# Sigmoid attention and a maxout block on one core: decodes in other visits, weight splits and two sums at other steps

## The chip, the cores and the metric

The program runs on one core of a Trainium2 chip. Times are microseconds (us) of device time; the result is the median of several runs. The engines are TensorE (PE), VectorE (DVE), ScalarE (ACT), GpSimd (POOL) and SyncE (SP), which issues nearly all DMAs from one queue, in order.

## The reference, cut to what matters

```python
scores = scale * np.matmul(q, k.transpose(0, 1, 3, 2)) - np.log(S)   # 8 batches, 12 heads, 448 x 64
attn = 1.0 / (1.0 + np.exp(-scores))
x = np.matmul(attn, v)            # laid out as 3584 tokens x 768
h = np.maximum(np.maximum(x @ w1, x @ w2), x @ w3)
return h @ w_out                  # all weights 768 x 768
```

## The kernel before, in words

Each engine works through its own list in the order in which the program writes it (`keep_in_program_order`), so an instruction that waits holds up everything behind it on its engine. All large products are made of float32 operands split into a high part (a ScalarE copy that rounds) and a low part (a VectorE subtraction, operand minus high part), and three matmuls take the place of one.

The program has three stretches. First comes the attention. Then come the three products of the maxout block, as Strassen-like products with twelve **visits** (`visits`, numbered here from 0): three rounds over four pairs of token blocks, the rounds using other quarters of the weights. A visit has 21 **steps** r, each one product of nine matmuls: seven products k for each of the three weights q, interleaved by the list `order` so that products k5 and k6 of one weight come after k0 of the next. `put` (L801) reads finished banks of PSUM: products k3 and k6 by a copy or a maximum, k4 and k5 by adding `p3`, which is VectorE work at L809, or at L814 and L815. Product k6 goes into the same bank as k4 and may only begin when k4's bank has been read; two products (k0 and k5 of others) lie between the two. Visit 0 has 19 steps.

Weights arrive in a coded form as 64-bit words. `decoding` (L196) loads three coded tiles ahead and turns one at a time into float32: two ScalarE passes (L220, L221) and four VectorE operations (L222, L226, L230, L231) by way of the tile `wb`, of which there is one. For rounds 1 and 2 the result is stored to DRAM by SP (L248), and the next decode's first VectorE operation cannot begin before this store has landed. The last twelve decodes, for the last layer's weights, write another tile and store nothing there. The table `decodes` (L778) says after which step of which visit a decode is written; `todo` says what is decoded in which order: first one tile for round 1 (which the load at visit 3, step 19 needs), then twelve for round 2 (the first four needed at visit 6), then twelve for the last layer. In the first four visits POOL makes the token sums of the next visit, some four us after another, beside this work.

The last stretch is the last layer, `h @ w_out`, with a scheme of 15 products (`STEPS`) of which each has two halves q of six matmuls; four pairs v of token blocks give 60 layer steps g. A product takes four blocks of 128x128 of the combined weights, 60 blocks in 20 tiles j of three blocks each, so layer step g < 15 needs tiles up to (4g+3)//3. Chains A, B and C of steps accumulate in the same banks without clearing them; `l_take` (L907) reads the bank after each step (L926 by ScalarE, L930 by VectorE), and the next step of the chain, often two steps later, must wait for that read. Token operands are h blocks b0 to B1, loaded by SP, and POOL sums of two (`X_SUMS`, 128x896; v's sums s0 to s16).

The work of the last layer is written by a plan with **places**: places 0 to 20 are the last 21 products (visit 11 from step 2 on), and layer step g is place 21 + g; a place's plan is written behind the product (places 0 to 20) or ahead of it (layer steps). In the plan stand, in this order: low part of a weight tile (`wl_lo`, L724), low part of a token operand (`l_lo`, L708), high part of one (`l_hi`, L698), POOL sums (`l_sum`, L676), loads (`l_load`, L671), high part of a weight tile (`wl_hi`, L720) and its load (L716). For layer step g the high part is written at place 18 + g and the low part at place 19 + g, but for those in the table EARLY; the operand goes into one of four sets, so the high part for step g waits until step g - 4 is done. `room` says for which steps ScalarE also copies the operand into the one PSUM buffer `ps_av` (L701), from which `l_lo` then reads instead of from SBUF. WL_SPLITS gives the place of each tile's high part; the low part follows one place later. `l_take_raw` (L658) hands out buffers for loads and sums from a list of free ones, by its order.

Of the kernel before, what the change touches and what calls it, by code (L numbers as in the profile page):

```python
# [101 lines left out]
def attention_then_maxout(  # L102
# [90 lines left out]
    def raw_tile(dec_p, name, words=HP):  # L193
        return dec_p.tile([P, words], I64, name=name, bufs=1)
# [457 lines left out]
    slots = ["xs_b11", "xs_t2", "xs_b12", "xs_b21", "xs_t1", "xs_t4", "xs_b22"]  # L652
# [3 lines left out]
    plan = {}  # L656

    def l_take_raw(key):  # L658
        name = slots.pop(0)
        if name[:2] == "wr":  # L660
            t = raw_tile(dec_p, name, S).bitcast(F32).rearrange("p (a s) -> p a s", s=S)
        elif name[:2] == "xs":
            t = xs_p[name == "xs_t4"].tile([P, HALF, S], F32, name=name)
        else:
            t = xo_p[1].tile([P, HALF, S], F32R, name=name).bitcast(F32)
        l_raw[key] = t[:, :2], name

    def l_load(v, name):
        l_take_raw((v, name))
        j, th = divmod(int(name[1]), 2)  # L670
        pin(nc.sync.dma_start(out=l_raw[v, name][0], in_=h_dram[v][:, th, j]))  # L671

    def l_sum(v, name):
        l_take_raw((v, name))
        a, b = (l_raw[v, x][0] for x in X_SUMS[name])
        pin(nc.gpsimd.tensor_tensor(out=l_raw[v, name][0], in0=a, in1=b, op=ALU.subtract))  # L676


    ROOM = (4, 7, 9, 10, 11, 12, 14, 0, 1)

    def room(v, s):
        return s in ROOM and (v or s > 4)

    def l_hi(v, s):
        g, x = v * len(STEPS) + s, l_raw[v, STEPS[s][1]][0]
        if g:
            name = SETS[(g - 1) % len(SETS)]
            to = xo_p[name not in FIRST]
            hi, lo = (
                to.tile([P, HALF, S], F32R, name=f"x{part}_{name}")[:, :2] for part in ("hi", "lo")  # L690
            )
        else:
            both = wl_p[0].tile([P, len(L_SUMS) * P], F32R, name="sums")
            hi, lo = (
                both[:, k * 2 * S : (k + 1) * 2 * S].rearrange("p (a s) -> p a s", a=2)
                for k in range(2)
            )
        pin(nc.scalar.copy(out=hi, in_=x))  # L698
        if room(v, s):
            px = ps_av.tile([P, 2, 512], F32, name="ps_av")  # L700
            pin(nc.scalar.copy(out=px[:, :, :S], in_=x))  # L701
            x = px[:, :, :S]
        l_ops[g], l_px[g] = (hi, lo), x
# [8 lines left out]
    def wl_load(j):  # L712
        q, k = divmod(j, len(PRODUCTS))
        wl_ops[j] = w_tiles(q, PRODUCTS[k][0])
        src = wl_dram[:].rearrange("p s b c -> p (s b c)")[:, j * HP : (j + 1) * HP]
        pin(nc.sync.dma_start(out=wl_ops[j][1].bitcast(F32), in_=src))  # L716
# [12 lines left out]
    for v in pairs:  # L729
        for s, (_, x, *_) in enumerate(STEPS):  # L730
            events.append((v, s - 3, 1, l_hi, s, (x,)))
            events.append((v, s - 2, 0, l_lo, s, () if room(v, s) else (x,)))
        events += [(v, s, 2, l_sum, x, X_SUMS[x]) for s, x in X_AT.items()]
        events += [(v, s, 3, l_load, x, ()) for s, xs_ in LOADS.items() for x in xs_]
# [4 lines left out]
        (l_load, "b5"): 5, (l_load, "b4"): 7,  # L739
        (l_sum, "s7"): 3, (l_sum, "s0"): 5, (l_sum, "s2"): 7, (l_sum, "s3"): 8,  # L740
        (l_sum, "s6"): 10, (l_sum, "s15"): 12,
        (l_hi, 0): 7, (l_hi, 1): 13, (l_hi, 2): 16, (l_hi, 3): 17, (l_hi, 4): 18,
        (l_lo, 0): 8, (l_lo, 1): 14, (l_lo, 2): 17, (l_lo, 3): 18, (l_lo, 4): 19,
    }

    def place(v, s, _, run, what, *rest):
# [18 lines left out]
    for k, e in enumerate(events):  # L765
        plan.setdefault(place(*e), []).append(lambda k=k: l_event(k))
    WL_LOADS = (1, 2, 3, 4, 5, 7, 8, 8, 9, 10, 11, 12, 14, 15, 15, 16, 17, 18, 19, 20)
    WL_SPLITS = (6, 7, 8, 9, 10, 11, 12, 13, 14, 15, 16, 17, 18, 19, 19, 20, 22, 24, 24, 26)
    for j, (at, split_at) in enumerate(zip(WL_LOADS, WL_SPLITS)):
        plan.setdefault(at, []).append(lambda j=j: wl_load(j))  # L770
        plan.setdefault(split_at, []).append(lambda j=j: wl_hi(j))
# [3 lines left out]
        for run in plan.get(at, ()):  # L775
            run()

    decodes = {n: (8, 11) if n < 3 else (6, 8, 10) for n in (1, 2, 3, 4, 5, 6, 8, 9, 10)}  # L778
    decodes = [(n, r) for n in decodes for r in decodes[n]]
    todo = [(1, 2, 3)] + [(2, q, n) for q in range(3) for n in range(4)]  # L780
    todo += [(STAGES, u, n) for u in range(2) for n in range(2 * HALF)]
# [39 lines left out]
    for at, (n, r, old, q, k) in enumerate(order):  # L821
# [21 lines left out]
        if here in his:  # L843
            to, name = his.pop(here)
# [8 lines left out]
        if here in x_loads:  # L853
            to, name = x_loads.pop(here)
# [87 lines left out]
    for g in range(end + 1):  # L942
        v, s = divmod(g, len(STEPS))
# [53 lines left out]
```

## Time and profile before

| | before |
|---|---|
| median of 3 runs | 857.94 us (857.68 to 858.5) |
| the profiled execution | 858.38 us, span 856.6 us, 1.8 us around it |
| PE busy | 846.0 us, 99% of the span, 5410 matmuls |
| VectorE, ScalarE, POOL busy | 618.7 us (72%), 510.5 us (60%), 238.8 us (28%) |
| chain that ended last | PE 95%, VectorE 4%, issue 1% |
| attention, visits, last layer | to 245.7 us, to 703.3 us, to 856.6 us |

PE's busy time includes matmuls that overlap in the pipeline; whether PE waited is seen from the starts of its matmuls, which follow one another at a fixed distance while nothing is late. A row of the timeline gives start, duration, engine, line, tiles and shapes, and in brackets the idle time before it with what ended it.

### The profile page before, as it was taken

Reading aid. Unit: us, or ns where it says so; the run is one execution under the profiler, and the core shown is the slowest. Engines: PE = TensorE matmul, PEld = TensorE weight load, DVE = VectorE, ACT = ScalarE, POOL = GpSimd, SP = SyncE. Lnnn points to the kernel's source line nnn. Section 1 sums busy time; section 2 is a strip of 40 time slices with the busy share of each in tenths; the row PEclk is TensorE's granted clock in tenths of the full one; section 3 lists DMA queues with packets and bytes.
Section 4 is the critical chain, followed back from the end, with each engine's and each line's share of the span. In section 5 each row is a group of like instructions: output and inputs, shape, how many; then the busy total and the mean of one; then the engine's idle time right before and its main releaser. Section 6 shows DMA issues by size and latency. Waiting matters only on the chain.

```text
span 856.6 us, 14461 instructions
## 1 busy us (share of the span) xinstructions
PE 846.0 (99%) x5410; PEld 699.0 (82%) x5410; DVE 618.7 (72%) x820; ACT 510.5 (60%) x717; POOL 238.8 (28%) x192
## 2 busy tenths in 40 slices
PE   9999999999999999999999999999999998999998
PEld 5555555555579989899999999999999987999997
DVE  5678668877883786875675765567576699898885
ACT  6888888888872444443364443345444445777774
POOL 0010020112017257204000230330303545578660
PEclk9999999999999999999999999999999999999999
DMA  8666777786666546446583922458382723735413
GB/s 295 209 211 228 252 247 232 259 298 239 196 248 224 205 177 226 180 124 210 196 268 116 326 71 66 163 197 281 123 294 67 249 90 126 237 132 190 151 65 129
DMA packets 79878, 166.95 MB, mean 195 GB/s; under 512 B 7616, under 2 KB 55744, under 8 KB 79808
## 3 DMA queue, kind: packets, MB, share of 16 engines
q1 hardware_dynamic: 79664, 165.92, 56.4%
q8 instruction: 42, 0.69, 0.3%
q14 instruction: 28, 0.23, 0.1%
q10 hardware_dynamic: 144, 0.11, 0.0%
HBM read 113.31 MB, written 52.69 MB: 194 GB/s over the span
## 4 chain that ended last, share of the span: by engine, by line
PE 95%; DVE 4%; issue 1%; DMA 0%; ACT 0%; DVEq 0%
PE ps_y L598 50%; PE ps_y L887 16%; PE ps_s L437 9%; PE ps_s L461 7%; PE ps_av L461 6%; PE ps_s L472 2%; PE ps_s L450 2%; PE ps_av L437 2%; DVE wb L226 1%; DVE wb L230 1%; DVE xlo_t L708 1%; DVE wb L231 0%; DMA w_dram<-wb 0%; PE ps_s L508 0%; DVE wb L222 0%
## 5 line engine op out<-in xcount | busy, mean ns | idle before, releaser
L799 ACT COPY ps_y<-ps_y 128x448 f32<-128x448 f32 x72 | 37.3, 518 | 170.1 <-PE ps_y L598 146.0
L407 ACT ACTIVATE a<-ps_s,bias_s 128x896 f32<-128x896 f32 x121 | 114.6, 1017 | 10.7 <-PE ps_s L437 10.7
L598 PE MATMUL ps_y<-xhi_t,whi_s 128*128 128x448 f32 x324 | 117.5, 363 | 0.0
L598 PE MATMUL ps_y<-xlo_t,whi_s 128*128 128x448 f32 x324 | 117.4, 362 | 0.0
L598 PE MATMUL ps_y<-xhi_t,wlo_s 128*128 128x448 f32 x324 | 116.8, 361 | 0.0
L178 POOL TENSOR_TENSOR ws_s<-ws_a,ws_a 128x384 f32<-128x384 f32 x9 | 9.7, 1080 | 285.7 <-DMA ws_a<-w_dram 180.1
L598 PE MATMUL ps_y<-xhi_b,whi_a 128*128 128x448 f32 x216 | 78.3, 362 | 0.0
L598 PE MATMUL ps_y<-xlo_b,whi_a 128*128 128x448 f32 x216 | 78.3, 362 | 0.0
L598 PE MATMUL ps_y<-xhi_b,wlo_a 128*128 128x448 f32 x216 | 78.0, 361 | 0.0
L598 PEld LDWEIGHTS ps_y<-xlo_t,whi_s 128*128 128x128 f32 x324 | 60.8, 188 | 4.4
L598 PEld LDWEIGHTS ps_y<-xhi_t,wlo_s 128*128 128x128 f32 x324 | 60.6, 187 | 4.2
L598 PEld LDWEIGHTS ps_y<-xhi_t,whi_s 128*128 128x128 f32 x324 | 60.8, 188 | 3.5
L461 PE MATMUL ps_av<-a,v 64*64 64x448 f32 x576 | 62.6, 536 | 0.0
L356 DVE TENSOR_TENSOR xlo_t<-xs_t,xhi_t 128x1344 fp32r<-128x1344 f32 x30 | 47.5, 1586 | 17.3 <-ACT xhi_t L352 15.4
L461 PE MATMUL ps_s<-a,v 64*64 64x448 f32 x576 | 59.7, 545 | 0.0
L814 DVE TENSOR_TENSOR c<-ps_y,p 128x448 f32<-128x448 f32 x48 | 29.8, 621 | 35.4 <-PE ps_y L598 35.3
L419 DVE TENSOR_TENSOR lo<-qk,hi 128x896 fp32r<-128x896 f32 (+4 forms) x51 | 53.5, 1049 | 1.8
L356 DVE TENSOR_TENSOR xlo_b<-xs_b,xhi_b 128x1344 fp32r<-128x1344 f32 x30 | 49.4, 1648 | 0.0
L352 ACT CAST xhi_t<-xs_t 128x1344 fp32r<-128x1344 f32 x30 | 39.6, 1320 | 15.1 <-PE ps_y L598 15.1
L461 PEld LDWEIGHTS ps_av<-a,v 64*64 64x64 f32 x576 | 22.0, 133 | 32.1 <-issue 32.1
L437 PE MATMUL ps_s<-hi 64*128 64x448 f32 x240 | 46.4, 384 | 0.0
L809 DVE TENSOR_TENSOR m<-ps_y,p 128x448 f32<-128x448 f32 x24 | 15.0, 624 | 42.0 <-PE ps_y L598 18.7
(214 smaller groups left out, 2225.4 us busy)
## 6 DMA issues: line engine op xcount, KB each, us to landing
qk<-qk SPq DMA_DIRECT2D x47, 448.0 KB, 4.7
xs_b<-x_dram SPq DMA_DIRECT2D x30, 672.0 KB, 6.4
wraw<-w SPq DMA_DIRECT2D x36, 384.0 KB, 4.5
xs_t<-t_dram SPq DMA_DIRECT2D x18, 672.0 KB, 6.9
v<-v SPq DMA_DIRECT2D x24, 448.0 KB, 5.5
h_dram<-m SPq DMA_DIRECT2D x48, 224.0 KB, 2.1
x_dram<-m SPq DMA_DIRECT2D x47, 224.0 KB, 2.9
t_dram<-xs_t SPq DMA_DIRECT2D x12, 672.0 KB, 3.8
```

The source lines that it names most:

```text
L352: pin(copy(out=hi, in_=r[name]))
L356: pin(nc.vector.tensor_tensor(out=lo, in0=x, in1=hi.bitcast(F32), op=ALU.subtract))
L407: pin(nc.scalar.activation(out=a, in_=banks[:, :, :S], func=AF.Sigmoid, bias=bias_s, scale=scale))
L419: pin(nc.vector.tensor_tensor(out=lo[:, cols], in0=t[:, cols], in1=high.bitcast(F32), op=ALU.subtract))
L437: pin(nc.tensor.matmul(bank[e][:, :S], kt[r, S + c * P : S + (c + 1) * P], qt[r, :S], start=n == 0, stop=n == len(terms) - 1,))
L450: pin(nc.tensor.matmul(ps[g * D : (g + 1) * D, e, :S], t[r, S + C * P :], t[r, :S], start=True, stop=True,))
L461: pin(nc.tensor.matmul(ps[e * D : (e + 1) * D, :S], vt[rows, (g * C + c) * 2 + e], chunks[c][rows, e], start=c == 0 and not (ahead and r = ...
L472: pin(nc.tensor.matmul(ps[e * D : (e + 1) * D, :S], vt[r, 4 * C + e], a[r, e], start=ahead[g], stop=not ahead[g],))
L598: pin(nc.tensor.matmul(ps[:, :S], wt[:, k * P : (k + 1) * P], xt[:, k], start=first and n == 0, stop=n == len(terms) - 1, skip_group_check ...
L799: pin(nc.scalar.copy(out=bank(cycle, b)[:, :S], in_=y[:, :S]))
L814: pin(nc.vector.tensor_tensor(out=c, in0=y, in1=add, op=ALU.add))
L887: pin(nc.tensor.matmul(ps[:, :S], wl_ops[j][part][:, c * P : (c + 1) * P], xt[:, k], start=first and m == 0, stop=m == len(terms) - 1, ski ...
```

## The change

Four edits in tables and one in the choice of buffers. No arithmetic changes; the number of decodes (25), of weight tiles (20) and of POOL sums stays.

- Decodes: visits 1 and 2 had two each, after steps 8 and 11. Now visits 0, 1 and 2 have one each, after steps 10, 8 and 8, and visit 5 has four (a new one after step 12). Visits 3, 4, 6, 8, 9 and 10 keep theirs.
- Weight tiles 0 to 13 of the last layer are split one or two places earlier; tiles 14 to 19 go from places 19 to 26 to places 28 to 33.
- The operand of layer step 0 is split one place earlier.
- For the first pair, steps 11 and 12 no longer copy their operand into PSUM.
- The sums s8 and s16 of the first pair take the buffer that was freed last, not first.

```diff
-        name = slots.pop(0)
+        name = slots.pop(-1 if key in ((0, "s8"), (0, "s16")) else 0)
...
-        return s in ROOM and (v or s > 4)
+        return s in (ROOM if v else (7, 9, 10, 14))
...
-        (l_hi, 0): 7, (l_hi, 1): 13, (l_hi, 2): 16, (l_hi, 3): 17, (l_hi, 4): 18,
-        (l_lo, 0): 8, (l_lo, 1): 14, (l_lo, 2): 17, (l_lo, 3): 18, (l_lo, 4): 19,
+        (l_hi, 0): 6, (l_hi, 1): 13, (l_hi, 2): 16, (l_hi, 3): 17, (l_hi, 4): 18,
+        (l_lo, 0): 7, (l_lo, 1): 14, (l_lo, 2): 17, (l_lo, 3): 18, (l_lo, 4): 19,
...
-    WL_SPLITS = (6, 7, 8, 9, 10, 11, 12, 13, 14, 15, 16, 17, 18, 19, 19, 20, 22, 24, 24, 26)
+    WL_SPLITS = (4, 5, 6, 7, 8, 10, 11, 11, 12, 13, 14, 15, 17, 18, 28, 29, 30, 31, 32, 33)
...
-    decodes = {n: (8, 11) if n < 3 else (6, 8, 10) for n in (1, 2, 3, 4, 5, 6, 8, 9, 10)}
+    decodes = {n: (6, 8, 10) for n in (3, 4, 5, 6, 8, 9, 10)}
+    decodes = {0: (10,), 1: (8,), 2: (8,), **decodes, 5: (6, 8, 10, 12)}
```

## Rows read from the trace of the kernel before

**Rows 1.** Windows without stall and behind the longest: us, busy (instructions) by engine, granted clock, DMA.

```profile
349.00:660.00 311.00, 311.00 (x1555) 291.51 (x1556) 202.64 (x288) 140.93 (x219) 51.28 (x80) 1.00 0.54 182
721.20:724.40 3.20, 3.20 (x9) 2.85 (x10) 3.20 (x5) 0.91 (x1) 1.80 (x1) 0.51 0.00 0
```

**Rows 2.** Timeline of PE at its six stalls: start, us, instruction, idle before.

```profile
308.57 0.36 PE L598 MATMUL ps_y<-xhi_t,whi_a 128*128 128x448 f32 x1
...
310.38 0.36 PE L598 MATMUL ps_y<-xlo_b,whi_s 128*128 128x448 f32 x1
...
347.79 0.37 PE L598 MATMUL ps_y<-xhi_t,whi_a 128*128 128x448 f32 x1
...
349.24 0.37 PE L598 MATMUL ps_y<-xlo_b,whi_s 128*128 128x448 f32 x1
...
689.05 0.37 PE L598 MATMUL ps_y<-xhi_t,whi_a 128*128 128x448 f32 x1
...
689.74 0.37 PE L598 MATMUL ps_y<-xlo_b,whi_s 128*128 128x448 f32 x1
...
700.14 0.37 PE L598 MATMUL ps_y<-xhi_t,whi_a 128*128 128x448 f32 x1
...
701.69 0.36 PE L598 MATMUL ps_y<-xlo_b,whi_s 128*128 128x448 f32 x1
...
707.89 0.37 PE L887 MATMUL ps_y<-xhi_b,whi_s 128*128 128x448 f32 x1
...
708.68 0.36 PE L887 MATMUL ps_y<-xlo_t,whi_s 128*128 128x448 f32 x1
...
718.08 0.36 PE L887 MATMUL ps_y<-xhi_t,wlo_s 128*128 128x448 f32 x1
721.10 0.60 PE L887 MATMUL ps_y<-xlo_t,whi_s 128*128 128x448 f32 x1 [2.65 <-DVE xlo_t L708]
...
724.79 0.37 PE L887 MATMUL ps_y<-xhi_t,whi_s 128*128 128x448 f32 x1
```

**Rows 3.** Timeline of VectorE, visit 1: second decode, then the late read of a bank.

```profile
304.30 0.36 DVE L222 TENSOR_SCALAR wb<-wraw 128x384 uint32<-128x384 uint32 x1 [2.05 <-DMA w_dram<-wb]
...
309.41 0.61 DVE L814 TENSOR_TENSOR c<-ps_y,p 128x448 f32<-128x448 f32 x1
```

**Rows 4.** Timeline of VectorE, visit 0: a long idle stretch.

```profile
265.82 0.62 DVE L811 TENSOR_TENSOR m<-ps_y,m 128x448 f32<-128x448 f32 x1 [6.63 <-PE ps_y L598]
```

**Rows 5.** Timeline of VectorE, visit 5: first and last operation of the third decode.

```profile
456.60 0.36 DVE L222 TENSOR_SCALAR wb<-wraw 128x384 uint32<-128x384 uint32 x1 [1.98 <-DMA w_dram<-wb]
...
458.28 0.56 DVE L231 SCALAR_TENSOR_TENSOR wb<-c,wb 128x384 f32<-128x384 f32 x1
```

**Rows 6.** Waits of VectorE for a store: us in total, times, longest.

```profile
DVE wb L222 <- DMA w_dram<-wb: 12.5, 6, 2.9
```

**Rows 7.** Timeline of VectorE, visit 11: reads of banks ahead of place 14.

```profile
686.36 0.61 DVE L811 TENSOR_TENSOR m<-ps_y,m 128x448 f32<-128x448 f32 x1
...
688.76 0.61 DVE L814 TENSOR_TENSOR c<-ps_y,p 128x448 f32<-128x448 f32 x1
```

**Rows 8.** Timeline of VectorE in the last layer: two-input operations, then one from PSUM.

```profile
715.66 2.49 DVE L724 TENSOR_TENSOR wlo_a<-wlo_a,whi_a 128x384 fp32r<-128x384 f32 x1
718.07 2.97 DVE L708 TENSOR_TENSOR xlo_t<-xs_t,xhi_t 128x896 fp32r<-128x896 f32 x1
...
722.03 1.08 DVE L708 TENSOR_TENSOR xlo_t<-ps_av,xhi_t 128x896 fp32r<-128x896 f32 x1
```

**Rows 9.** Timeline of POOL in the last layer: one sum under VectorE traffic, one alone.

```profile
715.29 2.44 POOL L676 TENSOR_TENSOR xlo_t<-wraw,xs_b 128x896 f32<-128x896 f32 x1
...
737.01 2.15 POOL L676 TENSOR_TENSOR xs_t<-xs_b,xhi_t 128x896 f32<-128x896 f32 x1 [10.12 <-ACT ps_av L701]
```

**Rows 10.** Timeline of ScalarE in the last layer: a high half.

```profile
714.03 0.96 ACT L698 CAST xhi_t<-xs_b 128x896 fp32r<-128x896 f32 x1
```

**Rows 11.** DMA issues: count, KB each, median us from issue to landing.

```profile
xs_b<-h_dram SPq DMA_DIRECT2D x10, 448.0 KB, 5.8
```

## The prediction

> **What bounds the kernel now.** I read the summary first: PE is busy for 99% of the span and the chain that ended last is PE for 95%, so only what makes PE wait counts. The view of windows shows what PE does when nothing is late: 1555 matmuls in 311.00 us, one every 0.200 us [rows 1]. A product of a visit (nine matmuls) is thus 1.80 us and a layer step (twelve) 2.40 us. Next I went through the starts of PE's matmuls from the end of the attention on and looked for distances over 0.22 us. There are six places, and each costs the distance from the last matmul before to the first one at full pace, less 0.200 for each interval between [rows 2]: in visits 1 and 2, 1.41 and 1.05 us; in visit 11 at places 14 and 20, 0.29 and 1.15; in the last layer ahead of step 2, 0.39, and inside step 6, 4.51 (11 intervals), where 2.65 us of idleness are followed by slow matmuls, at a granted clock of 0.51, the lower of its two levels, 1.2 GHz [rows 1]. Together 8.80 us. Everything else on PE is work that the change does not touch, so the floor is 857.94 - 8.80 = 849.1 us. All six waits end with a VectorE operation: five with the L814 or L811 that frees a bank, one with a token's low part. VectorE's list is what has to be followed.
>
> **Decodes.** In visit 1 the second decode begins at 304.30, 2.05 us after VectorE was ready, because the one `wb` was still being stored; L814, which frees the bank for k6, ends at 310.02 behind it, and PE starts at 310.07 [rows 2, 3]. Visit 2 repeats it. With one decode in these visits nothing stands between the first decode (done by 302.3) and L814, whose product ends at 305.2, two products ahead of the last matmul before k6: both waits go, -2.46. The decode that moves to visit 0, step 10 meets a VectorE that idles 6.63 us up to 265.82 [rows 4]. Beside POOL's sums, as in visit 1, a decode took at most the 4.6 us from 304.30 to the reads of banks ahead of 309.41 [rows 3], so it fits; were it a little late, L814's bank is due only 3.6 us after its product. Nothing, then; if that cover were gone, 1 us as in visit 2. Its store goes on SP's queue ahead of token stores that wait for POOL's sums anyway. The load that came with the decode at step 11 now comes at step 8 and has a whole visit to land.
>
> Visit 5 gets a fourth decode between k3's and k4's reads. The third decode ends at 458.84, and a decode takes 2.24 us from first to last [rows 5]. The gap ahead of the third decode, the wait for the second's store, was 1.98 [rows 5]; with it the fourth runs from 460.82 to 463.06, L814 (0.61 [rows 7]) follows to 463.67, and k6, due at 462.45 (63 products behind the one whose second matmul is that of 349.24 [rows 2]), starts at 463.7. With 0.1 for the restart as in the other stalls that is **+1.35**; bounds 0.9 (an overlap of the operations as dense as 0.48 us each) and 2.3 (a gap of 2.9, the longest of the six such waits [rows 6]). It is a wait for a DMA in VectorE's list, and behind it stand exactly the reads that PE needs. The Trainium skill's page "DMA: Bandwidth & Descriptors", section "Anatomy of one DMA", gives about 2.0 us fixed plus bytes over 436 GB/s for a DMA issued by GpSimd, an estimate of 2.45 for a store of 192 KB; by it the wait would be near 0.5 longer. The measured gap of 1.98 decides, and the sum keeps 1.35.
>
> **Visit 11.** ScalarE's and VectorE's weight splits for tiles 0 to 13 come earlier, tiles 14 to 19 go. Ahead of place 14, VectorE still has to do the same number of two-input operations (three low parts of weights and one of a token) in the time in which POOL makes its sums one after another, and each of them waits for the end of a running sum. What changes is that L811 now stands behind the last of them, not before: in the trace it ran at 686.36 while POOL held the next low part back anyway, and L814 began at 688.76 [rows 7]. Now L814 ends about 0.53 later, near 689.9 against a due time of 689.25: 0.70 + 0.11 = **0.81** in place of 0.29 (bounds 0.2 and 1.5). Behind it POOL is idle, as s8 is held back, three low parts of weights are missing, and L814 at place 20 ends 1 us early: the 1.15 and the 0.39 go.
>
> **The last layer.** This is where the change puts work, and the cover must be looked at. What the trace shows of VectorE beside POOL: a low part from PSUM takes 1.08 us whatever POOL does; one with both inputs in SBUF, of the same shape, took 2.97, and a 128x384 weight part 2.49 [rows 8]. Both ended just behind the end of a POOL sum: they start when the running sum ends, and POOL's next sum waits for them (2.44 under such traffic, 2.15 alone [rows 9]). So while POOL has sums ready, VectorE gets one two-input operation for each sum. The Trainium skill's "GPSIMD Engine Reference", section "Key points", says that the two share SBUF interfaces and contend where VectorE has two SBUF inputs; it has no price. It speaks against this change; without it the layer would have no wait.
>
> Let u be the time from the start of layer step 0. Step g is due at 2.4 g; the high part for g begins at 2.4 (g - 3) + 0.2 (0.96 [rows 10], then about as long for the copy into PSUM). Step 6 is safe now: its low part stands behind no weight part and ends at 9.9, due at 14.4: -4.51. But s8 now takes the buffer that ScalarE frees with the PSUM copy for step 7, at 12.0, and s16 that which the low part for step 8 frees, at 15.3 (VectorE first waits for s8 to end). POOL then has s16, s11, s5, s7, s0 and s2 (the last three for the next pair) in a row from 15.4, at about 2.1 each, into u = 30; in the trace this chain began before step 5. Into this stretch fall the low parts of tiles 14 to 19 and, without their PSUM copies, those for steps 11 and 12, and then 13. In order:
>
> - tile 14's high part follows the PSUM copy for step 10 and ends at 20.05; its low part waits for s5's end at 21.75. Then the low part for step 10 (PSUM) and two bank reads, to 24.3.
> - tile 15's low part gets in at s7's end, 24.2; the one for step 11 waits for s0's end, 26.6, and ends at 27.6; the bank read of step 9 follows. Step 11 starts at 28.2, due 26.4: 1.8 late.
> - tile 16 at 29.5; the one for step 12 from 29.95 to 31.0: 2.25 late. Between them POOL's next sum is not ready, as its load, issued at 24.8 behind the output of step 8, needs 5.8 [rows 11].
> - tile 17 behind that sum, 33.4, used at 32.85: 2.8 late; step 13's from 35.35 to 36.4: 5.25 late; tile 18 at 38.75, used at 37.65: 6.4 late; tile 19, whose high part waits for a PSUM copy that waits for step 14's low part, at 43.25, used at 40.6: **9.1 late**.
>
> After that no weight parts are left, and 7 us between high part and use absorb single waits as they did in the trace. The bounds of 9.1: 0.4 if VectorE finds POOL idle each time; 12.5 if tile 15 misses s7's end, which it makes by 0.1, so that all behind it slips by a sum. The clock may fall after a wait of over 2 us as it did after 2.65, but slow matmuls there mostly fill the next wait.
>
> **The sum**, against the profiled execution's 858.38: less 8.80, plus 1.35, 0.81 and 9.1, gives 860.84. The median of the runs is 0.44 below that execution, so I predict **860.4**. As a formula: 851.3 plus the layer's wait.
>
> **The rivals.**
> 1. VectorE's operations slip in between POOL's sums, at the 1.08 us or less that an undisturbed VectorE needs [rows 8], because the sums' loads or buffers come later than I think and leave gaps. Then the layer waits 0 to 4: 851.3 to 855.3, faster. It decides at the low part for step 11: if it is done by u = 26.4, this holds. For it: the trace has 7 us between high part and use and no wait of this kind in the later pairs, where POOL is as busy. Against it: there no weight parts stand in the list, and the critical steps have PSUM copies.
> 2. Some of the waits come and some not, above all if the loads for s3 and s6 of the next pair land later than 7 us and POOL pauses in steps 12 and 13: 4 to 8, 855.3 to 859.3.
> 3. All slips by one sum (tile 15 misses): 12.5 and perhaps a stretch at the low clock: 861.8 to 865.
> 4. The decode in visit 5 costs nothing, its store landing sooner: -1.35 on any of these. That the edits do not do what they say I exclude: they are tables.
>
> **How the numbers follow.** The forecast (8 to 10.5 in the layer, 859.3 to 861.8, its own range) has 0.33, rival 1 has 0.28, rival 2 0.22, rival 3 0.17. The range goes from 853.0, which leaves out about 0.12 of rival 1, to 864.0, which leaves out 0.04. A measurement of this kernel tells 0.2% (1.7 us) from no change; no change is thus 856.2 to 859.7. Slower: rival 3 and most of the forecast, 0.47. Same: a part of the forecast and most of rival 2, 0.20. Faster: rival 1 and the low end of rival 2, 0.33.
>
> **What would show it right or wrong.** In the changed kernel's trace: no stall in visits 0, 1 and 2; one of 1.2 to 1.5 us in visit 5 ahead of k6, ended by L814 with L222 behind a store; one near 0.8 at place 14 and none at place 20; none in layer step 6. POOL's sums s16 to s2 in one row across layer steps 6 to 12, and low parts of 2.4 and 3.0 us there; PE waiting for L708 and L724 in steps 11 to 14. I am wrong if POOL shows gaps in that stretch or if the low part for step 11 is done before step 10 ends.

## The result and the profile after

| | before | changed |
|---|---|---|
| median, in runs on the same chip | 857.81 us | 863.06 us (862.6 to 865.95) |
| ratio | | 1.0069, interval 1.0045 to 1.0093 |
| the profiled execution | 858.38 us, span 856.6 | 862.89 us, span 861.1 |
| PE's waits in visits 1 and 2 / visit 5 / place 14 / place 20 | 2.46 / 0 / 0.29 / 1.15 us | 0 / 1.10 / 0.95 / 0 us |
| PE's wait in the last layer | 4.90 us (steps 2 and 6) | 11.06 us (steps 11 to 14) |

The changed kernel is slower by 0.7%. PE's waits are those of the profiled execution. Lines have moved by one or two: L889 is the last layer's matmul (L887 before), L709 the low part of a token (L708), L725 that of a weight tile (L724), L816 the read of a bank with `p3` (L814), L932 the bank read of the layer (L930), L677 a POOL sum (L676), L702 the copy into PSUM (L701), L721 the high part of a weight tile (L720).

The timeline of PE at five of the stalls of the changed kernel, for each the last matmul ahead and the first behind, with what ended the wait in brackets: most lie in the last layer, and there a bank read, a token's low part and a weight's low part take turns. A stall costs the distance of the two starts, less 0.20, and about 0.1 for the restart:

```profile
460.00 0.36 PE L598 MATMUL ps_y<-xhi_t,whi_a 128*128 128x448 f32 x1
461.19 0.47 PE L598 MATMUL ps_y<-xhi_b,wlo_s 128*128 128x448 f32 x1 [0.83 <-DVE c L816]
...
687.90 0.37 PE L598 MATMUL ps_y<-xhi_t,whi_a 128*128 128x448 f32 x1
688.95 0.47 PE L598 MATMUL ps_y<-xhi_b,wlo_s 128*128 128x448 f32 x1 [0.68 <-DVE c L816]
...
727.86 0.37 PE L889 MATMUL ps_y<-xhi_t,whi_a 128*128 128x448 f32 x1
729.90 0.45 PE L889 MATMUL ps_y<-xhi_t,wlo_a 128*128 128x448 f32 x1 [1.68 <-DVE m L932]
...
732.39 0.37 PE L889 MATMUL ps_y<-xhi_b,wlo_s 128*128 128x448 f32 x1
734.62 0.47 PE L889 MATMUL ps_y<-xlo_b,whi_s 128*128 128x448 f32 x1 [1.86 <-DVE xlo_b L709]
...
745.47 0.58 PE L889 MATMUL ps_y<-xhi_t,whi_s 128*128 128x448 f32 x1
746.80 0.47 PE L889 MATMUL ps_y<-xhi_t,wlo_a 128*128 128x448 f32 x1 [0.76 <-DVE wlo_a L725]
```

460.00 to 461.19 is visit 5 (1.10), 687.90 to 688.95 place 14 (0.95). Layer step 0 starts at 701.66, so 729.90 is u = 28.24, the start of step 11, due at 26.4. Step 12 stops after its first matmul (732.39 to 734.62), and the last wait of the row, 746.80, is inside step 14, for tile 19; between the two lie further waits for tile 17, step 13 and tile 18, which are not shown. From there on every step is 11.06 us late and stays so. Nothing is late in visits 1 and 2, at place 20, or in layer steps 0 to 10. The remaining 0.2 us of the difference between the spans is that the visits start later, as the attention took longer in this execution.

VectorE in the last layer, beside POOL's sums (start, us, operation):

```profile
725.74 0.55 DVE L725 TENSOR_TENSOR wlo_s<-wlo_s,whi_s 128x384 fp32r<-128x384 f32 x1
726.21 3.02 DVE L709 TENSOR_TENSOR xlo_t<-xs_t,xhi_t 128x896 fp32r<-128x896 f32 x1
...
730.21 1.41 DVE L725 TENSOR_TENSOR wlo_s<-wlo_s,whi_s 128x384 fp32r<-128x384 f32 x1
731.54 3.02 DVE L709 TENSOR_TENSOR xlo_b<-xhi_t,xhi_b 128x896 fp32r<-128x896 f32 x1
734.49 2.46 DVE L725 TENSOR_TENSOR wlo_a<-wlo_a,whi_a 128x384 fp32r<-128x384 f32 x1
736.88 2.98 DVE L709 TENSOR_TENSOR xlo_b<-wraw,xhi_b 128x896 fp32r<-128x896 f32 x1
...
744.69 2.06 DVE L725 TENSOR_TENSOR wlo_a<-wlo_a,whi_a 128x384 fp32r<-128x384 f32 x1 [0.36 <-ACT whi_a L721]
```

```profile
723.30 2.45 POOL L677 TENSOR_TENSOR xhi_t<-wraw,xs_b 128x896 f32<-128x896 f32 x1
725.83 2.45 POOL L677 TENSOR_TENSOR xlo_t<-xhi_t,xlo_t 128x896 f32<-128x896 f32 x1
728.24 2.97 POOL L677 TENSOR_TENSOR xs_t<-wraw,xlo_t 128x896 f32<-128x896 f32 x1
731.17 2.45 POOL L677 TENSOR_TENSOR xs_b<-xlo_b,wraw 128x896 f32<-128x896 f32 x1
733.58 2.96 POOL L677 TENSOR_TENSOR wraw<-xs_b,xhi_b 128x896 f32<-128x896 f32 x1
736.62 2.30 POOL L677 TENSOR_TENSOR xs_b<-wraw,xhi_t 128x896 f32<-128x896 f32 x1
```

These are the rows that answer to [rows 8, 9]. 726.21 is the low part for layer step 11. POOL's sum had begun at 725.83 and ended at 728.28; the low part took 3.02 us and ended at 729.23, 0.95 behind the end of the sum; and POOL's next sum took 2.97 in place of the 2.15 of [rows 9], as it waited for the low part. The same happens at 730.21 (tile 16, up for the last 1.00 us of that sum), 731.54 (step 12), 734.49 (tile 17) and 736.88 (step 13). Only the tile 15 part at 725.74 found the gap between two sums and took 0.55. Here VectorE gets one such operation for each sum, as [rows 8] had suggested. The Trainium skill's "SBUF — State Buffer", section "SBUF: two separate sides", states a rule for this: of a VectorE instruction with two SBUF inputs and a GpSimd one that reads SBUF, whichever starts first has the shared access for the whole instruction, and the other is blocked fully. The trace agrees, to 0.13 us: 3.02 is the rest of the running sum, 2.07 (726.21 to 728.28), and 0.95 behind it, where the operation takes 1.08 undisturbed.

### The profile page after: what moved, and what is told of

Its sections match the earlier page's. It is cut to its first block, busy times and chain, and to the rows that moved or that the text cites. A ratio compares the mean times of both kernels' runs of the same rounds, so it can differ in the third digit from the quotient of the medians.

```text
span 861.1 us, 14454 instructions
## 1 busy us (share of the span) xinstructions
PE 848.9 (99%) x5410; PEld 700.2 (81%) x5410; DVE 618.8 (72%) x820; ACT 508.5 (59%) x715; POOL 240.0 (28%) x192
## 5 line engine op out<-in xcount | busy, mean ns | idle before, releaser
L816 DVE TENSOR_TENSOR c<-ps_y,p 128x448 f32<-128x448 f32 x48 | 29.9, 622 | 38.0 <-PE ps_y L598 36.9
L230 DVE CUSTOM_DVE_ANT_0 wb<-wraw,wb 128x768 uint16<-128x768 uint16 x48 | 28.6, 597 | 22.3 <-ACT wraw L221 18.7
```

Source lines behind the costliest of these rows:

```text
L230: pin(nc.vector.tensor_tensor(out=bits, in0=bits, in1=low, op=ALU.add))
L816: pin(nc.vector.tensor_tensor(out=c, in0=y, in1=add, op=ALU.add))
```

## The experiments

### The two halves of the change alone: d_only and l_only

d_only is the kernel before with the new decodes; l_only the changed kernel with the old ones.

```diff
-    decodes = {n: (8, 11) if n < 3 else (6, 8, 10) for n in (1, 2, 3, 4, 5, 6, 8, 9, 10)}
+    decodes = {n: (6, 8, 10) for n in (3, 4, 5, 6, 8, 9, 10)}
+    decodes = {0: (10,), 1: (8,), 2: (8,), **decodes, 5: (6, 8, 10, 12)}
```

d_only:

> Only the decodes move (one each in visits 0, 1 and 2, four in visit 5); the last layer is that of before. Both theories of the last layer expect the same here: the waits of visits 1 and 2 (1.41 and 1.05 us) are gone, one of about 1.1 to 1.35 stands in visit 5 ahead of k6, and the layer keeps its 0.39 and 4.51. Time: 857.8 - 2.46 + 1.1 to 1.35 = 856.4 to 856.7 us, ratio near 0.9985. A rival to the account of the fourth decode (its store lands in time and it costs nothing) expects 855.4.

l_only (all other edits of the change):

> Only the last layer's edits (splits, PSUM copies, buffers of s8 and s16); the decodes are those of before. If the parts add up: 857.8 plus 6.15 in the layer (11.06 in place of 4.91) and less 0.5 at places 14 and 20, 863.4 us, ratio near 1.0066. If the loss came from an interaction with the decodes, it is below 862.

Measured: d_only 855.68 us, ratio 0.9986 (0.9974 to 0.9997); l_only 864.08 us, ratio 1.0079 (1.0065 to 1.0094); the kernel before had 857.5 us in these runs. The loss is all in the last layer's edits. d_only's median is 1.8 us below that of the kernel before, which is more than the 1.1 to 1.4 expected, and not all of it is the edit's. Visits 1 and 2 have no stall and visit 5 has one of 1.88, not 1.1 to 1.35, so in this profile the decodes give 2.46 - 1.88 = 0.6. The two profiles lie 3.3 us apart (855.07 and 858.38): 1.6 of that is the clock, as the next rows show, 0.8 an attention that ended earlier, and 0.3 the stall of place 14, which is missing here. In l_only PE stands still in visits 1 and 2 (1.15 and 0.88), step 11 is 1.85 late and the layer's wait 12.71 us.

The profile of d_only shows one thing more, in layer step 6, which this edit does not touch. The timeline of PE, and the view of windows behind the stall (us, busy of PE, PEld, VectorE, ScalarE, POOL, granted clock, DMA share and GB/s):

```profile
716.40 0.37 PE L888 MATMUL ps_y<-xhi_t,wlo_s 128*128 128x448 f32 x1
719.38 0.47 PE L888 MATMUL ps_y<-xlo_t,whi_s 128*128 128x448 f32 x1 [2.62 <-DVE xlo_t L708]
719.69 0.37 PE L888 MATMUL ps_y<-xhi_t,whi_s 128*128 128x448 f32 x1
```

```profile
719.40:724.00 4.60, 4.60 (x23) 4.32 (x24) 4.60 (x8) 1.78 (x2) 2.91 (x2) 1.00 0.00 2
```

The wait for the low part is the same as in [rows 2], 2.62 us of idleness here and 2.65 there. But here the granted clock stays at 1.00 behind it, and the stall costs 2.89 us. In the trace of before the clock fell to 0.51 [rows 1] and the stall at the same matmul cost 4.51.

### What fills the gaps: e_calm, e_nopool and e_pop

Three kernels take one of the parties out of the collision. e_calm moves the six late weight splits to earlier places:

```diff
-    WL_SPLITS = (4, 5, 6, 7, 8, 10, 11, 11, 12, 13, 14, 15, 17, 18, 28, 29, 30, 31, 32, 33)
+    WL_SPLITS = (4, 5, 6, 7, 8, 10, 11, 11, 12, 13, 14, 15, 17, 18, 20, 21, 22, 22, 23, 24)
```

> The changed kernel with tiles 14 to 19 split at places 20 to 24 (20, 21, 22, 22, 23, 24) in place of 28 to 33, a stretch in which POOL now has no sums ready; s8 and s16 stay late, steps 11 and 12 stay without PSUM copies. The theory that each two-input VectorE operation waits out a POOL sum expects the layer's wait to fall from 11.06 to between 0 and 3 us: low parts of 0.55 us at places 21 to 25, step 11's low part at one sum's wait within its 7 us of cover; time 851.9 to 855, ratio 0.993 to 0.997. The theory that VectorE or ScalarE are simply too full in the layer, whatever POOL does (the same six splits have to be done), expects the wait to stay above 5 us, as before's 4.91: time over 857.

Measured: 852.15 us, ratio 0.9943 (0.9931 to 0.9955). PE does not wait in the last layer at all. VectorE's operations still wait for sums (the low parts for steps 11 and 13):

```profile
723.82 2.37 DVE L709 TENSOR_TENSOR xlo_t<-xs_t,xhi_t 128x896 fp32r<-128x896 f32 x1
...
729.05 3.02 DVE L709 TENSOR_TENSOR xlo_b<-wraw,xhi_b 128x896 fp32r<-128x896 f32 x1
```

They have 7 us between high part and use, and no weight part stands ahead of them, so nobody waits for them.

e_nopool leaves the splits late and takes the sums away:

```diff
+    BY_DMA = [(0, x) for x in ("s16", "s11", "s5")]
+    BY_DMA += [(1, x) for x in ("s7", "s0", "s2", "s3", "s6", "s15", "s9")]
...
     def l_sum(v, name):
         l_take_raw((v, name))
+        if (v, name) in BY_DMA:
+            pin(nc.sync.dma_start(out=l_raw[v, name][0], in_=h_dram[v][:, 0, 0]))
+            return
```

> The changed kernel with ten of POOL's sums left out (s16, s11 and s5 of the first pair, s7, s0, s2, s3, s6, s15 and s9 of the second): a load by SP fills their buffers in their place with other data, so that POOL is idle across layer steps 7 to 14 and all else stays, the six weight splits at places 28 to 33 too. The theory of POOL's sums expects low parts of 0.55 and 1.08 us there, no wait of PE over 0.5 us in steps 11 to 14 and a layer's wait of 0 to 1.5 us: time 852 to 853.5. The theory that VectorE's own work does not fit (2.6 us in steps of 2.4) or that ScalarE's casts come late behind the one PSUM buffer expects the wait for steps 11 to 14 to stay at 5 us or more: over 857.

Measured: 851.72 us, ratio 0.9940 (0.9927 to 0.9953). VectorE's list in the same stretch (L731 is the weight's low part, L715 the token's): tile 15, step 11, step 12:

```profile
723.46 0.55 DVE L731 TENSOR_TENSOR wlo_s<-wlo_s,whi_s 128x384 fp32r<-128x384 f32 x1
723.93 1.09 DVE L715 TENSOR_TENSOR xlo_t<-xs_t,xhi_t 128x896 fp32r<-128x896 f32 x1
...
726.46 1.09 DVE L715 TENSOR_TENSOR xlo_b<-xhi_t,xhi_b 128x896 fp32r<-128x896 f32 x1
```

The work on VectorE and ScalarE is the same, in the same order; without sums beside it the low parts take 1.09 in place of 3.02, and of 11.06 us of waiting 0.3 are left. So the rival that VectorE or ScalarE simply had too much to do in steps 11 to 14 falls.

e_pop leaves both and undoes the choice of buffers, so that the sums s8 and s16 come some 15 us earlier:

```diff
-        name = slots.pop(-1 if key in ((0, "s8"), (0, "s16")) else 0)
+        name = slots.pop(0)
```

> The changed kernel, but the sums s8 and s16 take the buffer that was freed first, as before. Theory (what delays the layer is that GpSimd's row of sums begins with s8 only at layer step 4 and then lies without a gap on steps 6 to 12): with both sums made 15 us earlier the row is over earlier or has gaps when the low parts of tiles 14 to 19 and of steps 11 to 14 come, and the layer's wait falls from 11.06 us to 2 to 6; the two sums lie beside visit 11 again and may bring back up to 1.1 us at place 20. Total 853 to 859. Rival (the buffers' order does not matter, as the loads set when the sums begin): 863 as before this undoing.

Measured: 856.54 us, ratio 1.0000 (0.9992 to 1.0009); the kernel before had 856.84 in these runs, as in those of e_px, e_six and best1. The row of sums now ends ahead of the critical stretch, and POOL then waits 6.99 us for a load; in this pause VectorE runs at full pace (tile 15, step 11):

```profile
731.60 2.96 POOL L677 TENSOR_TENSOR xs_t<-xs_b,xhi_t 128x896 f32<-128x896 f32 x1 [6.99 <-DMA xs_b<-h_dram]
```

```profile
727.01 0.55 DVE L725 TENSOR_TENSOR wlo_s<-wlo_s,whi_s 128x384 fp32r<-128x384 f32 x1
727.48 1.08 DVE L709 TENSOR_TENSOR xlo_t<-xs_b,xhi_t 128x896 fp32r<-128x896 f32 x1
```

The layer's wait is 2.59 us (0.39 at step 2 and 2.2 at tile 19, u = 36.68), and the stall at place 20 is back (0.6). So neither the late sums nor the late splits cost nearly as much alone: with early splits the late sums are harmless (e_calm), with early sums the late splits cost 2.2, and together they cost 11.06.

### The copies into PSUM: e_px, and the order on ScalarE: e_px_wf, e_wf

e_px gives steps 11 and 12 back their copy:

```diff
-        return s in (ROOM if v else (7, 9, 10, 14))
+        return s in (ROOM if v else (7, 9, 10, 11, 12, 14))
```

> The changed kernel, but ScalarE copies the operands of layer steps 11 and 12 of the first pair into PSUM again; the weight parts stay at places 28 to 33. Theory (VectorE gets one operation with two SBUF inputs in for each sum of GpSimd): the low parts for steps 11 and 12 take 1.08 us as with a PSUM input and no longer wait for a sum, so two of the slots go; the low parts of tiles 15 to 19 still wait for theirs. The layer's wait falls from 11.06 us to 4 to 8, total 855 to 860, and the first stall moves from step 11 to step 12 or 13. Rival (the two PSUM copies were a load on ScalarE and the one PSUM buffer a chain of its own, so leaving them out was a gain): the time stays at 863 or rises.

Measured: 861.72 us, ratio 1.007 (1.005 to 1.009). My theory was wrong on the time and on the first stall, which stays at step 11 (1.99 late); the rival has the total, as the ratio is that of the changed kernel (1.0069). The layer's wait is 11.27 us in the profile, of which 1.6 is slow matmuls behind the wait for tile 19. That wait itself ends 1.4 us sooner than in the changed kernel (u = 43.75 and 45.14), so the copies do spare VectorE something, but far less than I expected. VectorE and ScalarE around the low parts for steps 10 (725.82) and 11 (730.44):

```profile
725.82 1.08 DVE L709 TENSOR_TENSOR xlo_t<-ps_av,xhi_t 128x896 fp32r<-128x896 f32 x1
...
728.32 2.20 DVE L725 TENSOR_TENSOR wlo_s<-wlo_s,whi_s 128x384 fp32r<-128x384 f32 x1 [0.36 <-ACT whi_s L721]
730.44 1.08 DVE L709 TENSOR_TENSOR xlo_t<-ps_av,xhi_t 128x896 fp32r<-128x896 f32 x1
```

```profile
726.93 0.91 ACT L702 COPY ps_av<-xs_t 128x896 f32<-128x896 f32 x1 [2.21 <-DVE xlo_t L709]
727.78 0.51 ACT L721 CAST whi_s<-wlo_s 128x384 fp32r<-128x384 f32 x1
```

The low part for step 11 does take 1.08. But there is one PSUM buffer, so the copy at 726.93 waits for the low part for step 10 to end; the weight's high part (727.78) stands behind the copy on ScalarE; the weight's low part (728.32) waits for that, then for the running sum; and the next low part stands behind it. One turn of this ring takes 4.62 us, and the next 4.81, for steps of 2.40. The low parts without copies were 5.3 us apart (726.21, 731.54, 736.88 above).

e_px_wf tests that ring: in e_px, the high parts of tiles 14 to 19 are written ahead of the token's. e_wf is the same edit in the changed kernel.

```diff
-        plan.setdefault(split_at, []).append(lambda j=j: wl_hi(j))
+        plan.setdefault(split_at, []).insert(0 if j > 13 else 99, lambda j=j: wl_hi(j))
```

e_px_wf (the distances named in the text are those between the low parts for steps 10, 11 and 12; I had miscounted by one):

> The kernel with the PSUM copies for steps 11 and 12 restored, and in addition the high parts of tiles 14 to 19 written ahead of the token's high part and copy of the same place, not behind them. Theory (with the copies restored the layer waits for a ring of two engines: the copy waits for the last low part to leave the one PSUM buffer, the weight's high part stands behind the copy on ScalarE, the weight's low part waits for it on VectorE, and the next token's low part stands behind that): written first, the weight's high part waits for nothing, the distance between the low parts for steps 11, 12 and 13 falls from 4.6 and 4.8 us to 2.6 to 4, the layer's wait from 11.3 us to 3 to 7, total 853 to 858. Rival (GpSimd's sums alone hold VectorE back, whoever comes first on ScalarE): the distance stays at 4.5 to 5.3 and the time at 861 to 863.

e_wf:

> The changed kernel with the same edit alone: the high parts of tiles 14 to 19 ahead of the token's. Theory: steps 11 to 13 wait as before, as VectorE's list and GpSimd's sums are the same (1.8, 1.9 and 4.9 to 5.4 us late); only tile 19's low part, whose high part stood behind the copy for step 15, comes 1 to 2 us earlier, so that the layer's wait is 9 to 11 us in place of 11.06 and the total 860.5 to 862.5. Rival (ScalarE's order set those waits too): 855 to 858 with step 11 less than 1 us late.

Measured: e_px_wf 861.23 us, ratio 1.0042 (1.0027 to 1.0057); e_wf 863.09 us, ratio 1.0071 (1.0056 to 1.0086); the kernel before had 857.47. In e_px_wf the layer's wait is 9.77 us, not 3 to 7. The ring is broken once there: the low part for step 11 follows that for step 10 after 2.53 us, and step 11 is on time (1.99 late in e_px). Then tile 16's low part begins just behind the start of a sum. VectorE, and POOL's sum:

```profile
725.85 1.08 DVE L709 TENSOR_TENSOR xlo_t<-ps_av,xhi_t 128x896 fp32r<-128x896 f32 x1
...
727.90 2.53 DVE L725 TENSOR_TENSOR wlo_s<-wlo_s,whi_s 128x384 fp32r<-128x384 f32 x1
730.36 1.08 DVE L709 TENSOR_TENSOR xlo_b<-ps_av,xhi_b 128x896 fp32r<-128x896 f32 x1
```

```profile
727.89 2.13 POOL L677 TENSOR_TENSOR xs_t<-wraw,xlo_t 128x896 f32<-128x896 f32 x1
```

It takes 2.53, and the low part for step 12 is 4.51 behind that for step 11. The wait for tile 19 ends at u = 42.02 (43.75 in e_px, 45.14 in the changed kernel), so each of the two edits gives something, but the sums hold VectorE back with ScalarE's order changed too, and the total is the rival's. In e_wf the layer's wait is 11.11 us and the total 0.6 above the expected range. There tile 19's part does come up 0.4 us earlier than in the changed kernel (u = 42.66 and 43.03), but it comes up at the very moment at which POOL begins its next sum. VectorE and POOL:

```profile
743.77 2.49 DVE L725 TENSOR_TENSOR wlo_a<-wlo_a,whi_a 128x384 fp32r<-128x384 f32 x1
```

```profile
743.77 2.08 POOL L677 TENSOR_TENSOR wraw<-xs_b,xlo_b 128x896 f32<-128x896 f32 x1
```

POOL had the sum done in 2.08, VectorE took 2.49; the gain that I expected is lost to one slot missed. The wait for tile 19 ends at u = 45.20.

### The decode in visit 5: e_six

```diff
-    decodes = {0: (10,), 1: (8,), 2: (8,), **decodes, 5: (6, 8, 10, 12)}
+    decodes = {0: (10,), 1: (8,), 2: (8,), **decodes, 6: (6, 8, 10, 12)}
```

> The changed kernel, but the fourth decode stands in visit 6 after step 12, not in visit 5. From visit 6 on most decodes are for the last layer and write no store that the next one waits for. Theory: the stall in visit 5 (1.10 us in the profile of the changed kernel, 1.4 to 1.9 in three others) goes and none comes in visit 6; total 861.2 to 862.0, 1 to 2 below the changed kernel in the same runs. Rival (four decodes do not fit between k3 and k6 whatever they wait for): a stall of 0.5 to 2 us in visit 6 in its place, total near 863.

Measured: 862.49 us, ratio 1.0072 (1.0058 to 1.0087), 0.5 above the theory's range. The stall of visit 5 is gone and visit 6 has none; visit 4, which the edit does not touch, has one of 0.26 here (0.55 in e_pop), and what sets it I did not find out. Visit 6 on VectorE: the end of the third decode, the start of the fourth, the bank read behind it:

```profile
493.33 0.56 DVE L231 SCALAR_TENSOR_TENSOR wd<-c,wb 128x384 f32<-128x384 f32 x1
...
494.34 0.35 DVE L222 TENSOR_SCALAR wb<-wraw 128x384 uint32<-128x384 uint32 x1
...
496.49 0.62 DVE L816 TENSOR_TENSOR c<-ps_y,p 128x448 f32<-128x448 f32 x1
```

The fourth decode begins right behind the third and a bank read (493.33 to 494.34), with no store between them. The total does not show the gain: in this profile the layer's wait is 13.29 us, which the next runs explain.

### The changed kernel once more: after_again

> The changed kernel once more, to see how much of its layer's wait is the same in each execution. Step 11 is 1.8 to 1.9 us late as in the first profile and step 12 1.9; the sum of the layer's wait lies between 11 and 13.5, as it lay in three kernels with the same last layer; total 861.5 to 864.5.

Measured: 863.99 us, ratio 1.0080 (1.0053 to 1.0107); in the profile step 11 is 1.84 late, step 12 1.93, and the layer's wait is 13.32 us, 2.26 more than in the first profile. The wait for tile 19 ends at the same moment in every kernel with this last layer: u = 45.14, 45.19 (this one), 45.22 (l_only), 45.23 (e_six), and also in e_wf, 45.20. What differs is the granted clock behind it. Windows of the first profile (during the waits; behind the last), then of this one (behind the last), columns as in [rows 1]:

```profile
736.30:746.00 9.70, 8.32 (x20) 5.50 (x18) 9.34 (x9) 2.19 (x3) 9.62 (x5) 0.50 0.26 95
746.80:752.00 5.20, 5.20 (x26) 4.88 (x27) 4.71 (x6) 4.22 (x7) 0.00 (x0) 1.00 0.46 174
```

```profile
747.00:751.60 4.60, 4.60 (x13) 4.08 (x14) 3.94 (x5) 3.11 (x5) 0.00 (x0) 0.50 0.39 149
```

In the first profile the low clock (0.50) lies on the stretch in which PE waits for VectorE anyway, and behind the last wait PE runs at the higher of its two levels: 26 matmuls in 5.20 us. Here the low clock also lies behind the last wait: 13 matmuls in 4.60 us in place of 23, so ten are missing at 0.20 each, nearly the whole 2.26 us. What VectorE alone makes of the layer's wait is thus the same 11.1 us in all five profiles, to 0.1, and the clock adds 0 to 2.2.

### All three remedies: best1

```diff
-    WL_SPLITS = (4, 5, 6, 7, 8, 10, 11, 11, 12, 13, 14, 15, 17, 18, 28, 29, 30, 31, 32, 33)
+    WL_SPLITS = (4, 5, 6, 7, 10, 10, 11, 11, 12, 13, 14, 15, 17, 18, 20, 21, 22, 22, 23, 24)
...
-    decodes = {0: (10,), 1: (8,), 2: (8,), **decodes, 5: (6, 8, 10, 12)}
+    decodes = {0: (10,), 1: (8,), 2: (8,), **decodes, 6: (6, 8, 10, 12)}
```

> The changed kernel with three things altered: tiles 14 to 19 split at places 20 to 24, the fourth decode in visit 6, and tile 4 split at place 10, not 8. Theory: all three stalls that the changed kernel has left (visit 5, place 14, layer steps 11 to 14) are gone, the starts of the matmuls have no gap behind the attention, and the time is the floor of the prediction, 849.1 (849.0 to 850.5), ratio to the kernel before 0.990 to 0.991. Rival (one of the waits comes back elsewhere, at place 14 or in layer steps 3 to 6): 851 to 853.

Measured: 849.14 us, ratio 0.9918 (0.9906 to 0.9931), faster than both kernels. The view of PE's waits has one row left, in the attention, which the kernel before has too:

```profile
PE ps_s L508 <- PEq L987: 0.8, 1, 0.8
```

No start of a matmul behind the attention is late by more than a restart. 849.14 is also the floor that the prediction worked out by taking all stalls off (849.1). That the two agree to 0.1 is partly luck: the kernel before had 856.84 in these runs, and the same 8.80 taken off that gives 848.0.

## Why the prediction was right, and where it was short

The sign, the places and the mechanism were right, and 863.06 lies within the range (853.0 to 864.0), in the bracket of rival 3. The range is 11 us wide, so that alone says little: the forecast's own range (859.3 to 861.8) was missed, and one of the four executions, 865.95, lies above both. The point was 2.66 us low. By its own steps:

- **Visits 1 and 2, visit 0.** No stall is left in any of them, in d_only neither. In visit 0 the working had a decode of at most 4.6 us; it took 6.91 (259.34 to 266.25), as VectorE waited 3.62 in it for a ScalarE pass (L221). It just fit: the bank read behind it began at 266.17, against 265.82 before [rows 4].
- **Visit 5: 1.35 forecast, 1.10 measured.** The timeline of VectorE, here and at place 14:

```profile
455.81 0.56 DVE L231 SCALAR_TENSOR_TENSOR wb<-c,wb 128x384 f32<-128x384 f32 x1
...
458.36 0.36 DVE L222 TENSOR_SCALAR wb<-wraw 128x384 uint32<-128x384 uint32 x1 [1.45 <-issue]
...
460.52 0.62 DVE L816 TENSOR_TENSOR c<-ps_y,p 128x448 f32<-128x448 f32 x1
...
685.36 2.47 DVE L725 TENSOR_TENSOR wlo_s<-wlo_s,whi_s 128x384 fp32r<-128x384 f32 x1
...
688.29 0.61 DVE L816 TENSOR_TENSOR c<-ps_y,p 128x448 f32<-128x448 f32 x1
```

The fourth decode begins at 458.36, 1.99 us behind the end of the third (456.37; the bank read of k3 lies in between, so the row shows 1.45 of idleness, and the view names no releaser for it; that it is the store I take from the equal gap of [rows 5], where the view names it, and from e_six). The decode takes 2.24, and L816 stands behind it. Each term is as forecast; what moves is when the decodes begin against PE. Eight other profiles with this decode gave 1.26 to 2.23, all but one above the forecast; I did not find out what sets that. e_six shows the stores' part: in visit 6 the fourth decode between the same reads has no store ahead of it, nor has the third, and no stall follows. The measured 1.99 is the gap of [rows 5]. By the fit of the Trainium skill's "DMA: Bandwidth & Descriptors", section "Anatomy of one DMA", which is for DMAs issued by GpSimd, a store of this size is an estimate of 2.45 us; here SP issues it, and the trace has 1.99 from the end of one decode to the start of the next.
- **Place 14: 0.81 forecast, 0.95 measured.** L813 and L816 stand behind two weight parts of 2.5 us each, as said. The nine other profiles with these early splits gave 0.17 to 1.31, so that the forecast is met this closely is luck. Place 20 and step 2 are on time, as said.
- **Layer step 6** is on time, as said.
- **The layer's wait: 9.1 forecast, 11.06 measured.** Up to step 11 the working held to a few tenths, forecast and measured u: s8 begins at 12.0 and 12.12, s16 at 15.4 and 15.36, tile 14 is done at 21.75 and 22.09, tile 15 comes up at 24.2 and 24.08, the low part for step 11 ends at 27.6 and 27.57, step 11 starts at 28.2 and 28.24. Tile 16: 29.5 and 29.96. Then the low part for step 12: **31.0 forecast, 32.90 measured**. From there on all is late by the same sum: tile 17 at 33.4 and 35.29, step 13 at 36.4 and 38.20, tile 18 at 38.75 and 40.61, tile 19 at 43.25 and 45.09.

So one step failed: "POOL's next sum is not ready, as its load ... needs 5.8". The DMA issues of that stretch (count, KB, us from issue to landing):

```profile
xlo_b<-h_dram SPq DMA_DIRECT2D x1, 448.0 KB, 4.1
```

The load was issued at u = 24.57 (forecast 24.8) but took 4.1 us, not the 5.8 of [rows 11]. It landed at 28.7, before the sum ahead of it was over (29.55), so POOL made no pause, and its next sum began at 731.17, ahead of the low part for step 12 at 731.54. That low part waited for the sum, 3.02 in place of 1.08. The same load took 3.7 to 4.9 us in l_only, e_six, after_again and e_wf, and POOL made no pause in any of them. The trace of before could have said so: it has seven groups of loads of this size from `h_dram`, by buffer, with medians of 4.2 to 5.8, and the prediction took the longest. This is the group of the buffer in which the load lands (view and columns of [rows 11]):

```profile
xlo_b<-h_dram SPq DMA_DIRECT2D x2, 448.0 KB, 4.2
```

That a later load would have saved the 1.9 us is worked out from these rows; no run delays it alone. This is rival 3's mechanism (all behind a missed slot slips by one sum), but the slot missed was not tile 15's.

- **The clock.** "Slow matmuls there mostly fill the next wait" held in the profiled execution. Other executions show 0 to 2.2 us on top, which the sum did not hold. Nor was "a wait of over 2 us" what decided: in d_only the clock stayed at 1.00 behind 2.62 us of idleness, and in e_px it was 0.50 behind 1.96 in visit 5, where ten slow matmuls cost another 1.6.
- **The sum.** With the measured terms, 849.58 + 1.10 + 0.95 + 11.06 = 862.7, against 862.89. Of the 2.66 that the point was low, 1.96 is the layer, nearly all of it that one missing pause; the decode and place 14 together take 0.11 off. Another 0.61 is that I put the median 0.44 below the profiled execution, as it was before, while now it is 0.17 above it. What is left, 0.2, is mostly the start of the visits.
- **Rival 1** fell by its own criterion (the low part for step 11 was done at u = 27.57, not by 26.4). e_nopool and e_pop show that it was right on what decides: where POOL pauses, VectorE is undisturbed and the layer's wait falls to 0.3 and 2.6. **Rival 4** did not come about in any profile with four decodes in visit 5.

## What to carry to other kernels

Where VectorE takes two operands from SBUF beside a row of GpSimd operations, count one VectorE operation per GpSimd operation, not by their own durations, and look for slots that are missed by tenths of a microsecond: a missed one delays all behind it. Before moving work "later, where it is needed", look at what else becomes dense there: two edits that cost 2.2 us (late splits, with early sums) and nothing (late sums, with early splits) made 11 us together. Look at all groups of loads of the size in question, not at one median, and when a chain depends on a pause of another engine, keep the case without the pause as an end of the range.

## What was not expected of the hardware

The stall in layer step 6 cost 4.51 us in the kernel before and 2.89 in d_only, after waits of 2.65 and 2.62, and what differs is the granted clock behind it (0.51 and 1.00); the same layer cost 11.06 and 13.32. Where the low clock falls against the waits was not settled: no run here controls it. The kernels with little or no waiting in the last layer (best1, e_calm, e_nopool, e_pop) show the clock at 1.00 there, to the end, in their profiles.

With a copy into PSUM the token's low part took 1.08 us beside running sums too, yet the copy hardly helped (e_px): with one buffer it ties ScalarE to VectorE, and the ring's 4.6 to 4.8 us were nearly as bad as the 5.3 us of two sums.
